# Grouped 1x1 convolution on one core: VectorE block transposes and an in-place ring in place of TensorE transposes and two rings

## The chip, the cores and the metric

The kernel runs on one core of one Trainium2 chip. The metric is the device time of one execution in microseconds (us). Executions of one kernel mostly agree closely: the four of the kernel before took 491.78 to 493.43 us. So differences of 1% are visible when several rounds are run. A run more than 1.5% above the fastest of the same kernel counts as slow. Only fast runs are compared.

The engines are PE (TensorE; PEld is its weight load), DVE (VectorE), ACT (ScalarE), POOL (GpSimd) and SP (the queue that issues loads). A trailing q, as in ACTq, is an engine's sequencer.

## The reference

Every pixel has 192 channels in 4 groups of 48. Each group is multiplied by its own 48x48 matrix. With k = 1 there is no padding and no sum over neighbours:

```python
H = W = 512; G = 4; Cg = 48; C = 192; k = 1
x: (1, 512, 512, 192) bfloat16      w: (1, 1, 4, 48, 48) bfloat16
out = einsum('bhwgc,gcd->bhwgd', x.reshape(1, 512, 512, 4, 48), w[0, 0])
```

The input is 100.66 MB and the output as much. A "column" below is 128 pixels, one per partition: 49,152 bytes in and as many out; there are 2048 columns.

## The kernel before

Pixels lie on partitions. The kernel contracts over partitions, so it first brings the channels there. TensorE does it, by multiplying with an identity; DVE copies the result from PSUM to SBUF; a second set of matmuls multiplies by the weights; ACT (and DVE for one eviction in eight) brings the output to SBUF. Work goes in groups of 4 columns. Loads and stores go in pieces of 64 columns, smaller ones at head and tail. Input and output each have a ring of 256 columns.

```python
BIG = 64; RCOLS = 256
HEAD = (4, 4, 8, 16, 32); TAIL = (32, 16, 8, 4, 4)
...
x_sb = sbuf_tensor([128, RCOLS * C]); o_sb = sbuf_tensor([128, RCOLS * C])
...
for p in loads:                                  # SP
    wq.wait(t_done, p.g1 - body)                 # the slot's old input is transposed
    sp.dma_start(ring_view(x_sb, p), rows_view(xf, p))
...
pe.transpose(xT_ps[:, g % NXP, j * 128:(j + 1) * 128], x_sb[:, col:col + 128], ident[:])   # 6 a group
dve.tensor_copy(xT_sb[g % NXP][:], xT_ps[:, g % NXP, 0:2 * UC])
pe.matmul(o_ps[:, v % NOB, c0_:c1_], lhsT=xs[:, j * 128:(j + 1) * 128], rhs=wt[...])       # 6 a group
...
wait_out_free(wq, g)                             # the slot's old output is stored
act.copy(dst, o_ps[:, v % NOB:v % NOB + 2, 0:UC])
```

## Time and profile before

| | before |
|---|---|
| time, median | 492.5 us |
| span of the profiled run | 489.8 us |
| bytes moved | 201.63 MB |
| GB/s from 100 to 400 us | 431 |
| PE / DVE / ACT busy | 86 / 69 / 73% |

These lines are from the page of the kernel before: busy us of each engine, GB/s in 40 equal slices of the span, the DMA total, and the costliest groups of instructions. A group's line gives the source line, engine and operation, what was written from what, the count, then busy us and mean ns of one, then the engine's idle time just before them and what ended it.

```profile
PE 423.4 (86%) x6154; PEld 407.9 (83%) x6154; DVE 336.1 (69%) x640; ACT 357.2 (73%) x513; POOL 1.3 (0%) x8
...
GB/s 297 430 425 423 428 430 433 427 435 425 436 425 432 433 431 433 429 432 431 425 433 430 429 435 429 434 429 433 429 429 426 438 421 434 421 424 351 238 385 149
DMA packets 11750, 201.63 MB, mean 412 GB/s; under 512 B 1488, under 2 KB 2512, under 8 KB 3536
...
L277 ACT CAST o_sb<-o_ps 128x768 bf16<-128x768 f32 x385 | 301.7, 799 | 116.8 <-PE o_ps L215 68.4
L249 DVE COPY xT_sb<-xT_ps 128x768 bf16<-128x768 bf16 x512 | 284.0, 555 | 111.4 <-PE xT_ps L192 104.4
L215 PE MATMUL o_ps<-wt,xT_sb 128*128 128x144 bf16 (+1 forms) x3072 | 308.2, 238 | 47.9 <-ACT o_sb L277 44.8
L192 PE MATMUL xT_ps<-ident,x_sb 128*128 128x128 bf16 x3072 | 265.7, 225 | 7.8 <-DMA x_sb<-in_x_dram 7.3
...
L255 DVE CAST o_sb<-o_ps 128x384 bf16<-128x384 f32 x127 | 69.8, 550 | 28.0 <-DMA out_dram<-o_sb 26.7
```

After its first slice the GB/s row is flat at about 430 until its last four slices: this kernel is bound by DMA nearly all the way. The chain of waits says the same; this is its summary by line:

```profile
by line: DMA out_dram<-o_sb 73.5%; PE o_ps L215 10.3%; PE xT_ps L192 7.7%; DMA x_sb<-in_x_dram 3.7%; ACT o_sb L277 1.1%; another core or an unknown queue 0.8%; issue 0.6%; SPq L164 0.4%; ACTq L264 0.1%; SPq L161 0.1%; ACTq L46 0.0%
```

The next lines are stretches of the trace before. The columns are the stretch, then for each engine busy us and number of instructions, then the granted TensorE clock, the DMA engines' mean busy share, and GB/s.

```profile
core 0: us, PE busy (x) PEld busy (x) DVE busy (x) ACT busy (x) POOL busy (x), PEclk, DMA share, GB/s
0.00:20.00 20.00, 14.93 (x176) 13.79 (x177) 10.34 (x19) 8.77 (x12) 1.31 (x8) 1.00 0.90 348
100.00:400.00 300.00, 259.70 (x3767) 251.51 (x3765) 206.01 (x393) 217.73 (x315) 0.00 (x0) 0.95 1.00 431
400.00:440.00 40.00, 36.26 (x535) 35.14 (x533) 29.09 (x57) 30.54 (x45) 0.00 (x0) 0.96 1.00 426
440.00:450.00 10.00, 10.00 (x158) 9.76 (x156) 8.36 (x17) 9.00 (x14) 0.00 (x0) 1.00 0.96 399
450.00:460.00 10.00, 9.27 (x143) 8.85 (x141) 8.23 (x16) 8.70 (x13) 0.00 (x0) 1.00 0.80 335
460.00:470.00 10.00, 9.65 (x149) 9.40 (x149) 7.46 (x15) 8.15 (x12) 0.00 (x0) 1.00 0.43 180
470.00:480.00 10.00, 5.88 (x71) 5.26 (x69) 3.53 (x7) 4.61 (x7) 0.00 (x0) 0.85 0.77 323
```

201.63 MB at 431 GB/s take 468 us. The rest of the span is lost in the first 20 us and after 440 us. In that tail PE is nearly always busy until 473 us. Two lines of the same kernel's timeline of PE (start us, duration us, instruction, and in brackets the idle time before it) show: PE stood still for 3.94 us at the very end, for a load.

```profile
472.74 0.58 PE L215 MATMUL o_ps<-wt,xT_sb 128*128 128x144 bf16 x6
477.25 0.82 PE L192 MATMUL xT_ps<-ident,x_sb 128*128 128x128 bf16 x6 [3.94 <-DMA x_sb<-in_x_dram]
```

### The profile page before, as it was taken

The page shows a single profiled execution, that of the slowest core. Times are in us where ns is not written, and L with a number is a line of the kernel's source. Part 1 is how long each engine was busy: PE and PEld are TensorE (multiplying, and loading weights), DVE is VectorE, ACT ScalarE, POOL GpSimd, SP SyncE. Part 2 cuts the span into 40 slices and gives each one's busy share as a digit, 9 for nine tenths or more (in the row PEclk, how much of TensorE's full clock was granted, in tenths as well). Part 3 has the DMA queues.
Part 4 walks back from the last instruction along what each step waited for, and adds up shares of the span by engine and source line. Part 5 has one row for each costly group of instructions (what it writes and reads, how often), then busy time and mean ns, then how long its engine had stood idle before and what let it go on. Part 6 is the DMA issues. An engine that isn't in the chain of part 4 may idle for free.

```text
span 489.8 us, 14171 instructions
## 1 busy us (share of the span) xinstructions
PE 423.4 (86%) x6154; PEld 407.9 (83%) x6154; DVE 336.1 (69%) x640; ACT 357.2 (73%) x513; POOL 1.3 (0%) x8
## 2 busy tenths in 40 slices
PE   5999989977997979979798979899798979799962
PEld 5899989977987879878788878898787978799862
DVE  3688878867675767757676757767577757588750
ACT  2788878866785767767677757678586868688862
POOL 1000000000000000000000000000000000000000
PEclk9999999999898998989998989989899989899996
DMA  8999999999999999999999999999999999998593
GB/s 297 430 425 423 428 430 433 427 435 425 436 425 432 433 431 433 429 432 431 425 433 430 429 435 429 434 429 433 429 429 426 438 421 434 421 424 351 238 385 149
DMA packets 11750, 201.63 MB, mean 412 GB/s; under 512 B 1488, under 2 KB 2512, under 8 KB 3536
## 3 DMA queue, kind: packets, MB, share of 16 engines
q1 hardware_dynamic: 5968, 100.68, 48.3%
q10 hardware_dynamic: 5760, 100.67, 48.2%
q8 instruction: 12, 0.20, 0.1%
q14 instruction: 10, 0.08, 0.0%
HBM read 100.68 MB, written 100.66 MB: 411 GB/s over the span
## 4 chain that ended last, share of the span: by engine, by line
DMA 77%; PE 18%; ACT 1%; another core or an unknown queue 1%; issue 1%; SPq 1%; ACTq 0%
DMA out_dram<-o_sb 73%; PE o_ps L215 10%; PE xT_ps L192 8%; DMA x_sb<-in_x_dram 4%; ACT o_sb L277 1%; SPq L164 0%; ACTq L264 0%; SPq L161 0%; ACTq L46 0%
## 5 line engine op out<-in xcount | busy, mean ns | idle before, releaser
L277 ACT CAST o_sb<-o_ps 128x768 bf16<-128x768 f32 x385 | 301.7, 799 | 116.8 <-PE o_ps L215 68.4
L249 DVE COPY xT_sb<-xT_ps 128x768 bf16<-128x768 bf16 x512 | 284.0, 555 | 111.4 <-PE xT_ps L192 104.4
L215 PE MATMUL o_ps<-wt,xT_sb 128*128 128x144 bf16 (+1 forms) x3072 | 308.2, 238 | 47.9 <-ACT o_sb L277 44.8
L192 PE MATMUL xT_ps<-ident,x_sb 128*128 128x128 bf16 x3072 | 265.7, 225 | 7.8 <-DMA x_sb<-in_x_dram 7.3
L215 PEld LDWEIGHTS o_ps<-wt,xT_sb 128*128 128x128 bf16 x3072 | 217.8, 100 | 61.4 <-issue 52.5
L192 PEld LDWEIGHTS xT_ps<-ident,x_sb 128*128 128x128 bf16 x3072 | 205.6, 101 | 9.5 <-DMA x_sb<-in_x_dram 7.6
L255 DVE CAST o_sb<-o_ps 128x384 bf16<-128x384 f32 x127 | 69.8, 550 | 28.0 <-DMA out_dram<-o_sb 26.7
L274 ACT CAST o_sb<-o_ps 128x384 bf16<-128x384 f32 x127 | 61.0, 480 | 8.0 <-PE o_ps L215 5.1
L245 DVE CAST wt<-o_ps 128x480 bf16<-128x480 f32 x1 | 0.7, 658 | 3.2 <-PE o_ps L176 3.2
L176 PE MATMUL o_ps<-w_sb,esel 48*128 48x48 bf16 x10 | 0.6, 210 | 2.6 <-DMA w_sb<-in_w_dram 2.6
L176 PEld LDWEIGHTS o_ps<-w_sb,esel 48*128 48x128 bf16 x10 | 0.5, 112 | 2.5 <-POOL esel L150 2.5
L277 ACT ACT_TABLE_LOAD x1 | 1.3, 1283 | 0.8 <-PEq L300 0.8
L150 POOL TENSOR_SCALAR_AFFINE_SELECT esel<-esel 48x272 bf16<-48x272 bf16 x1 | 0.4, 406 | 0.0
L147 POOL MEMSET esel<- 48x272 bf16 x1 | 0.3, 318 | 0.3 <-POOLq L300 0.3
L154 POOL TENSOR_SCALAR_AFFINE_SELECT ident<-ident 128x128 bf16<-128x128 bf16 x1 | 0.3, 285 | 0.0
L148 POOL MEMSET ident<- 128x128 bf16 x1 | 0.2, 198 | 0.0
L300 POOL MEMSET const-bfloat16-1.0<- 128x1 bf16 x1 | 0.1, 102 | 0.0
L300 POOL MEMSET const-uint8-127<- 128x1 uint8 x1 | 0.1, 102 | 0.0
L300 POOL MEMSET const-float32-0.0<- 128x1 f32 x1 | 0.1, 98 | 0.3 <-issue 0.3
L300 POOL MEMSET const-float32-1.0<- 128x1 f32 x1 | 0.1, 98 | 0.0
## 6 DMA issues: line engine op xcount, KB each, us to landing
x_sb<-in_x_dram SPq DMA_DIRECT2D x30, 3072.0 KB, 25.7
out_dram<-o_sb ACTq DMA_DIRECT2D x30, 3072.0 KB, 45.4
x_sb<-in_x_dram SPq DMA_DIRECT2D x2, 1536.0 KB, 19.7
out_dram<-o_sb ACTq DMA_DIRECT2D x2, 1536.0 KB, 24.9
x_sb<-in_x_dram SPq DMA_DIRECT2D x2, 768.0 KB, 21.5
out_dram<-o_sb ACTq DMA_DIRECT2D x2, 768.0 KB, 20.0
x_sb<-in_x_dram SPq DMA_DIRECT2D x4, 192.0 KB, 27.2
x_sb<-in_x_dram SPq DMA_DIRECT2D x2, 384.0 KB, 24.4
```

The costliest lines, as they stand in the source:

```text
L147: gp.memset(esel[:], 1.0).then_inc(p0_sem, 1)
L150: gp.affine_select(out=esel[:], in_=esel[:], pattern=[[-1, ECOLS]], compare_op=AluOpType.is_equal, fill=0.0, base=ESHIFT, channel_multipli ...
L154: gp.affine_select(out=ident[:], in_=ident[:], pattern=[[-1, 128]], compare_op=AluOpType.is_equal, fill=0.0, base=0, channel_multiplier=1) ...
L176: last = pe.matmul(o_ps[:, NOB - 1, col:col + CG], lhsT=esel[:, s0:s0 + 128], rhs=w_sb[:, g, :], start=True, stop=True, skip_group_check=True)
L192: ins.append(pe.transpose(xT_ps[:, g % NXP, j * 128:(j + 1) * 128], x_sb[:, col:col + 128], ident[:]))
L215: ins.append(pe.matmul(o_ps[:, v % NOB, c0_:c1_], lhsT=xs[:, j * 128:(j + 1) * 128], rhs=wt[:, WOFF[tc]:WOFF[tc] + (c1_ - c0_)], start=(tc ...
L245: dve.tensor_copy(wt[:], o_ps[:, NOB - 1, 0:WCOLS]).then_inc(wc_sem, 1)
L249: dve.tensor_copy(xT_sb[g % NXP][:], xT_ps[:, g % NXP, 0:2 * UC]).then_inc(e1_sem[g % RING], 1)
L255: dve.tensor_copy(o_sb[:, u * UC:(u + 1) * UC], o_ps[:, v % NOB, 0:UC]).then_inc(d2_sem[g // 4 % 2], 1)
L274: ins = act.copy(o_sb[:, u * UC:(u + 1) * UC], o_ps[:, v % NOB, 0:UC])
L277: ins = act.copy(dst, o_ps[:, v % NOB:v % NOB + 2, 0:UC])
L300: nc = _bacc.Bacc("TRN2", target_bir_lowering=False, num_devices=1)
```

## The change

The intent was to take the transposes off TensorE and their PSUM evictions off DVE. DVE transposes 32x32 blocks from SBUF to SBUF. The kernel is laid out for blocks that stay within 32 partitions, so that each quarter of the partitions keeps its own pixels. The weights therefore become block-diagonal, one copy per quarter, and the 128 PSUM partitions come to mean "pixel run i*4+u". For a store to see those partitions in address order, the transposed columns must be ordered (i, u): the transpose writes its 32 outputs of a block four elements, 8 bytes, apart. Outputs overwrite their inputs in one ring of 512 columns, and a load waits for the store 512 columns earlier.

```diff
-BIG = 64
-RCOLS = 256
-HEAD = (4, 4, 8, 16, 32)
-TAIL = (32, 16, 8, 4, 4)
+STEP = 8
+BIG = 128
+RCOLS = 512
+HEAD = (8, 8, 16, 32, 64)
+TAIL = (64, 32, 16, 8, 8)
 ...
+            for p in pieces:                                    # SP
+                for q in pieces:
+                    if q.col < p.col + p.size - RCOLS and q.col + q.size > p.col - RCOLS:
+                        wq.wait(st_sem[q.i], 16)
+                sp.dma_start(region(p), pixels(xf, p).rearrange("(p i) c -> p (i c)", p=128))
 ...
-                        ins.append(pe.transpose(xT_ps[...], x_sb[:, col:col + 128], ident[:]))
-                    dve.tensor_copy(xT_sb[g % NXP][:], xT_ps[:, g % NXP, 0:2 * UC])
+                src = columns(s).rearrange("p u g (b j) -> p u (g b) j", j=Q)           # Q = 32
+                dst = xT[s % NXT][:].rearrange("p (b i u) -> p u b i", u=NQ, i=Q)       # NQ = 4
+                dve.transpose(dst, src).then_inc(t_done, 1)
 ...
+                for gh in range(4):                             # PE: 12 matmuls a step
+                    for b, o, r in ((1, ...), (0, ...), (2, ...)):
+                        pe.matmul(o, lhsT=xs[:, at:at + 128], rhs=r, start=(b == 1), stop=(b == 2))
 ...
+                dst = pixels(of, p).rearrange("(a q g) c -> q a (g c)", a=NQ, q=128)    # store: 4 runs
+                src = region(p).rearrange("p (a n) -> p a n", a=NQ)                     # a partition
+                act.dma_start(dst, src).then_inc(st_sem[p.i], 16)
+                act.copy(columns(s)..., o_ps[...])              # output over its input
```

## The prediction

> What bounds it now. DMA, then a compute tail. The stretches of the trace show 431 GB/s from 100 to 400 us, DMA share 1.00, and the chain of waits is 73% out_dram<-o_sb. The page counts 201.63 MB; at 431 GB/s that is 468 us of the 489.8 us span. The other 22 us: about 4 us in the first 20 us (348 GB/s) and about 17 us after 440 us (399, 335, 180, 323, 170 GB/s in 10 us stretches). In that tail the loads are over and the chain is PE alone, 6 transposes (0.33 us) and 6 matmuls (0.41 to 0.47 us) per group of 4 columns, 0.78 us a group until 473 us. The backlog exists because compute had been held back by the full output ring (ACT waited 46.9 us and DVE 26.7 us for stores), so about 40 loaded groups were left uncomputed when loads ended.
>
> What the change does, per step of 8 columns (1024 pixels; 256 steps). DMA needs 0.786 MB / 431 GB/s = 1.83 us.
> - Removed: 12 TensorE transposes and two PSUM-to-SBUF copies on DVE (555 ns each), shared evictions (550 ns).
> - DVE: one transpose of 128x1536 bf16. No such instruction is in the trace. [...] 256 x 1.78 = 456 us: DVE goes from 69% to about 95% busy and nearly ties with DMA.
> - PE: 12 matmuls, 3072 columns; the trace's pace (960 columns in 0.41 us) gives 1.32 us, 338 us in all.
> - ACT: one eviction of 128x1536. From 480 ns for 384 and 799 for 768, 1.44 us, 368 us in all. Two PSUM halves: (1.32+1.44)/2 is far under 1.83, so no PSUM stall.
> - In-place ring: the output overwrites the input, so compute never waits for a store; only loads do (store of the piece 512 columns earlier). Bytes unchanged.
>
> On the critical path. The middle stays DMA-bound (no gain). The gain is the tail: compute follows the loads closely, some 280 columns wait in the store queue when loads end, and they drain at DMA rate while the last 100 to 250 columns are computed. I expect the tail's loss to fall from 17 us to about 5, while the head costs 1 to 4 us more (first piece twice as large, weights built by four small DMAs and four ACT copies before the first matmul). Span: 468 + 4 + 5 = 477 us, plus 2 to 3 us between span and time: 480 us, ratio 0.974.
>
> Chances: faster 0.60, same 0.24, slower 0.16; 80% range 474 to 500.
>
> What would show it. DVE transposes of about 1.78 us, DVE over 90% busy; ACT mean 1.44 us; PE under 75%; no ACT or DVE wait for out_dram; 425 to 433 GB/s in the middle, and over 350 GB/s in all but the last 10 us. If DVE is the limit instead, GB/s falls evenly below 425 in the middle, and the chain is DVE transposes.
>
> What would make it wrong. A transpose over 1.85 us (its output is scattered with an 8-byte step[...], this trace shows nothing of it): each 0.1 us is 26 us. A lower DMA rate from 12 KB store runs and 48 KB row pitch. Piece-wise starvation of a DVE with only about 3% slack. Late weights holding DVE after its four buffers.

In the line on DVE the sum came to 1.78 us for one transpose, 1.7 to 1.85 us from start to start. The 1.78 us, and with it the 456 us, the 95% and the 3% of slack, stand as the author's estimate, with no measurement behind it. The sum of the span, 468 + 4 + 5 = 477 us, assumes that DVE keeps up with DMA, but has no term for it.

## The result, and the profile after

| | before | after |
|---|---|---|
| time, median | 492.5 us | 896.8 us |
| span of the profiled run | 489.8 us | 895.0 us |
| ratio of the fast runs | 1 | 1.821 (1.818 to 1.824) |
| DVE busy | 69% | 98% |
| PE busy | 86% | 50% |

A ratio is the mean time of one kernel's fast runs over the mean of the other's in the same rounds, so it is not quite the ratio of the medians. The change is much slower, not 2.6% faster. These lines of the page after answer to those of before:

```profile
PE 445.0 (50%) x3072; PEld 290.0 (32%) x3072; DVE 874.9 (98%) x256; ACT 371.2 (41%) x261; POOL 1.9 (0%) x6
...
GB/s 385 427 413 252 211 71 388 106 282 282 141 385 38 351 212 192 362 10 389 174 236 327 53 396 114 282 282 97 396 70 299 264 149 133 1 281 1 192 186 185
...
L138 DVE STREAM_TRANSPOSE xT<-ring 128x1536 bf16<-128x1536 bf16 x256 | 874.9, 3635 | 14.0 <-PE o_ps L160 10.2
L160 PE MATMUL o_ps<-wt,xT 128*128 128x192 bf16 (+1 forms) x3072 | 445.0, 303 | 445.4 <-DVE xT L138 412.2
L190 ACT CAST ring<-o_ps 128x1536 bf16<-128x1536 f32 x256 | 367.9, 1438 | 510.7 <-PE o_ps L160 488.7
```

The mean of one transpose is 3635 ns, and 874.9 us busy for 256 of them is 3.42 us from one start to the next. (Where DVE never idles, busy time over count is the time from start to start; adjacent instructions overlap a little, so it is below the mean.) The author's estimate was 1.78 us. The chain of waits by line and the longest waits tell one story, that everything waits for DVE; a wait's columns are total us, number of times, longest us:

```profile
by line: DVE xT L138 91.8%; issue 3.1%; ACTq L184 2.5%; PE o_ps L160 0.8%; DVEq L90 0.6%; ACT ring L190 0.5%; DMA ring<-in_x_dram 0.3%
```

```profile
ACT ring L190 <- PE o_ps L160: 488.7, 250, 3.2
...
PE o_ps L160 <- DVE xT L138: 412.2, 246, 1.9
...
DVE xT L138 <- PE o_ps L160: 10.2, 1, 10.2
```

256 x 3.42 us are 875 us. The rest of the 895 us span is 3.7 us before the first transpose, 10.2 us in which DVE waited for PE, and the last step's matmuls, eviction and store. DMA falls to 211 GB/s in the middle, because it has nothing more to do:

```profile
0.00:60.00 60.00, 22.99 (x132) 14.95 (x132) 51.34 (x15) 16.07 (x14) 1.93 (x6) 0.76 0.98 413
60.00:100.00 40.00, 25.61 (x157) 16.60 (x158) 34.68 (x11) 20.93 (x15) 0.00 (x0) 0.76 0.79 320
100.00:400.00 300.00, 182.81 (x1056) 114.53 (x1054) 300.00 (x88) 127.10 (x89) 0.00 (x0) 0.76 0.51 211
```

The 10.2 us have a cause of their own. These are lines of ACT's timeline after: one store's issue took 23.44 us where others took 0.38 us. ACT stood still for 22.05 us with it; PE waited up to 19.4 us for ACT to evict its PSUM, and DVE 10.2 us for PE to free a buffer.

```profile
22.98 0.38 ACTq L184 DMA_DIRECT2D out_dram<-ring  x1
...
37.50 23.44 ACTq L184 DMA_DIRECT2D out_dram<-ring  x1
60.98 2.78 ACT L190 CAST ring<-o_ps 128x1536 bf16<-128x1536 f32 x2 [22.05 <-issue]
```

In the first 60 us the two queues (q1 loads, q10 stores) moved this (packets, MB, share):

```profile
q1 hardware_dynamic: 1122, 24.48, 96.5%
q10 hardware_dynamic: 614, 0.29, 1.7%
```

Load packets are some 22 KB each here (24.48 MB over 1122), store packets about 0.5 KB (0.29 MB over 614; the weights' packets are among them).

### The profile page after: what moved, and what is told of

Same layout as the page of the kernel before. It is cut to its first block, busy times and chain, and to the rows that moved or that the text cites. A ratio compares the mean times of both kernels' runs of the same rounds, so it can differ in the third digit from the quotient of the medians.

```text
span 895.0 us, 7034 instructions
## 1 busy us (share of the span) xinstructions
PE 445.0 (50%) x3072; PEld 290.0 (32%) x3072; DVE 874.9 (98%) x256; ACT 371.2 (41%) x261; POOL 1.9 (0%) x6
## 4 chain that ended last, share of the span: by engine, by line
DVE 92%; issue 3%; ACTq 2%; PE 1%; DVEq 1%; ACT 0%; DMA 0%
DVE xT L138 92%; ACTq L184 2%; PE o_ps L160 1%; DVEq L90 1%; ACT ring L190 0%; DMA ring<-in_x_dram 0%
## 5 line engine op out<-in xcount | busy, mean ns | idle before, releaser
L138 DVE STREAM_TRANSPOSE xT<-ring 128x1536 bf16<-128x1536 bf16 x256 | 874.9, 3635 | 14.0 <-PE o_ps L160 10.2
L160 PE MATMUL o_ps<-wt,xT 128*128 128x192 bf16 (+1 forms) x3072 | 445.0, 303 | 445.4 <-DVE xT L138 412.2
L190 ACT CAST ring<-o_ps 128x1536 bf16<-128x1536 f32 x256 | 367.9, 1438 | 510.7 <-PE o_ps L160 488.7
L160 PEld LDWEIGHTS o_ps<-wt,xT 128*128 128x128 bf16 x3072 | 290.0, 107 | 600.2 <-DVE xT L138 474.8
L176 ACT COPY wt<-w_sb 32x384 bf16<-32x384 bf16 x4 | 2.0, 510 | 0.1
```

Source lines behind the costliest of these rows:

```text
L138: dve.transpose(dst, src).then_inc(t_done, 1)
L160: ins = pe.matmul(o, lhsT=xs[:, at:at + 128], rhs=r, start=(b == 1), stop=(b == 2), skip_group_check=True)
L176: act.copy(dst, w_sb[:]).then_inc(wc_sem, 1)
L190: act.copy(dst, src).then_inc(o_done, 1)
```

## The experiments

Two questions were open. Why does a transpose cost 3.42 us? And would the rest of the prediction have held, had it cost what was expected? The first seven experiments, all on the transpose, and the one on the head after them give a wrong result, since moving columns about spoils the matmul's order; the bytes moved and the work of the other engines are those of a real run. The diffs below show only the lines that matter.

### The transpose: step, operation, size

**Unit step.** The only edit is the order of the output columns:

```diff
-dst = xT[s % NXT][:].rearrange("p (b i u) -> p u b i", u=NQ, i=Q)
+dst = xT[s % NXT][:].rearrange("p (u b i) -> p u b i", u=NQ, i=Q)
```

> Edit: the transpose writes its output in one contiguous run (order u, b, i) instead of with an 8-byte step; the result is wrong on purpose. Theory S[...]: the transpose falls from 3.4 us start to start to about 1.8 us and the time to about 480 to 500 us. Theory T[...]: stays within 3% of 3.4 us, time about 895 us.

Theory S lays the 3.4 us on the step of the output; theory T lays it on the 32x32 transpose of 2-byte elements, whatever its patterns.

Time 497.9 us (one run). The group of DVE in this run:

```profile
L138 DVE STREAM_TRANSPOSE xT<-ring 128x1536 bf16<-128x1536 bf16 x256 | 425.8, 1736 | 42.9 <-PE o_ps L160 36.0 <-DMA ring<-in_x_dram 6.9
```

425.8 us over 256 is 1.66 us, 1.08 ns per element, where the change took 3.42 us, 2.22 ns. Theory T, that a transpose takes the longer time whatever its pattern, falls. The output's step is what doubled the cost.

**A plain copy with the change's own patterns.**

```diff
-dve.transpose(dst, src).then_inc(t_done, 1)
+dve.tensor_copy(dst, src).then_inc(t_done, 1)
```

> Edit: a plain DVE copy with the very same source and destination patterns in place of the transpose; wrong result on purpose. Theory S: about 3.4 us each, time about 895 us. Theory T: about 1.6 to 1.8 us each[...], and the time then shows what the rest of the change is worth with a DVE instruction of the predicted size: the prediction's 480 us if its account of the ring and the tail is right, more if they cost something.

Time 500.2 us (one run).

```profile
L138 DVE COPY xT<-ring 128x1536 bf16<-128x1536 bf16 x256 | 442.0, 2044 | 39.4 <-PE o_ps L160 34.1 <-DMA ring<-in_x_dram 5.2
```

1.73 us each, 1.12 ns per element. So the plain form of theory S falls as well: a copy that writes 8 bytes apart takes about as long as the transpose with a unit step. It takes the step and the transpose together.

**Half of the blocks**, with the same 8-byte step:

```diff
-src = columns(s).rearrange("p u g (b j) -> p u (g b) j", j=Q)
-dst = xT[s % NXT][:].rearrange("p (b i u) -> p u b i", u=NQ, i=Q)
+src = columns(s)[:, :, 0, :].rearrange("p u (b j) -> p u b j", j=Q)
+dst = xT[s % NXT][:, 0:XT // 2].rearrange("p (b i u) -> p u b i", u=NQ, i=Q)
```

> Edit: each step transposes only the first of its two pixel groups, 24 of 48 blocks, 768 elements per partition, with the same 8-byte step; wrong result on purpose. [...] If half of the 3.4 us were a fixed cost of one instruction, about 2.6 us. With DVE at about 1.8 us, the time tests the rest of the prediction: 480 us if it is right.

The forecast, for a cost that goes by elements, was about 1.8 us start to start.

Time 501.1 us (one run).

```profile
L141 DVE STREAM_TRANSPOSE xT<-ring 128x768 bf16<-128x768 bf16 x256 | 440.4, 1915 | 40.2 <-PE o_ps L164 34.4 <-DMA ring<-in_x_dram 5.8
```

1.72 us for 768 elements against 3.42 us for 1536: 1.70 us for 768 more, 2.21 ns per element, which leaves 0.02 us fixed. (This run also zeroes the unused half of each buffer once, at the start.)

**The same bytes as 4-byte elements:**

```diff
-src = columns(s).rearrange("p u g (b j) -> p u (g b) j", j=Q)
-dst = xT[s % NXT][:].rearrange("p (b i u) -> p u b i", u=NQ, i=Q)
+src = region(piece_of[s]).bitcast(F32)...rearrange("p u g (b j) -> p u (g b) j", j=Q)
+dst = xT[s % NXT][:].bitcast(F32).rearrange("p (b i u) -> p u b i", u=NQ, i=Q)
```

> Edit: the same bytes transposed as 768 4-byte elements (pairs of channels stay together; wrong result on purpose, as the matmuls are not adapted). [...]: about 1.8 us. If the cost goes by bytes: about 3.4 us. [...]: about 1.0 us. The output's step grows from 8 to 16 bytes[...].

Two forecasts are for an element that costs as much at 4 bytes as at 2 (1.8 us), and for one that costs half as much (1.0 us); theory S expected no less than the first.

Time 497.9 us (one run).

```profile
L140 DVE STREAM_TRANSPOSE xT<-ring 128x768 f32<-128x768 f32 x256 | 376.1, 1556 | 87.8 <-PE o_ps L162 39.4 <-DMA ring<-in_x_dram 37.8
```

Here DVE waits for others, so busy over count, 1.47 us, is an upper bound. Ten in a row span 13.99 us in the trace; less the last one's own 1.56 us (the mean), that is 1.38 us from start to start, some 1.80 ns for each of 768 elements. The step is 16 bytes here, and a 4-byte element costs less than a 2-byte one at 8 bytes (2.22 ns). None of the three expectations fits exactly, and the distance in bytes alone does not explain the cost.

**A step of 2 elements**, 4 bytes (u split into v and w, output ordered b, v, i, w):

```diff
+src = columns(s).rearrange("p (v w) g (b j) -> p v w (g b) j", v=2, j=Q)
+dst = xT[s % NXT][:].rearrange("p (b v i w) -> p v w b i", w=2, v=2, i=Q)
```

> Edit: the transpose writes its output with a step of 2 elements (4 bytes) in place of 4 (8 bytes); wrong result on purpose. Found so far: 1.66 us start to start with step 1, 3.42 us with step 4, a plain copy with step 4 1.72 us. Theory U[...]: 3.4 us, time about 895 us. Theory L (the cost follows how far apart consecutive writes lie[...]): clearly less than 3.4 us, between 1.7 and 2.6 us, time 500 to 700 us.

Theory U is that only a unit step is fast, and any other costs as much as the step of 4.

Time 502.3 us (one run); 446.7 us over 256 is 1.74 us, 1.14 ns per element. A unit step is not needed; theory U falls.

```profile
L138 DVE STREAM_TRANSPOSE xT<-ring 128x1536 bf16<-128x1536 bf16 x256 | 446.7, 1918 | 39.7 <-PE o_ps L160 34.5 <-DMA ring<-in_x_dram 5.0
```

**A step of 8 elements**, 16 bytes, for the transpose and for the plain copy:

```diff
+src = columns(s)...rearrange("p u (c e) j -> p u c e j", e=2)
+dst = xT[s % NXT][:].rearrange("p (c i e u) -> p u c e i", e=2, u=NQ, i=Q)
```

> Edit: the transpose writes with a step of 8 elements (16 bytes), in the patterns of the change otherwise; wrong result on purpose. Known: step 1 1.66 us start to start, step 2 1.74 us, step 4 3.42 us. If the cost doubles[...]: near 6.5 us, time near 1700 us. [...]: 3.4 us, time about 895 us.

> Edit: a plain copy with the step of 8 elements (16 bytes) in place of the transpose; wrong result on purpose. The copy took 1.72 us at a step of 4 elements. If a step of more than 4 elements slows every DVE write, and the transpose only has half the tolerance: about 3.4 us, time about 895 us. If the step matters to the transpose alone: 1.7 us, time about 500 us.

The forecast for the transpose, 3.4 us, is for one that loses no more beyond a step of 8 bytes.

The transpose ran in 1756.0 us, the copy in 896.7 us (one run each).

```profile
L138 DVE STREAM_TRANSPOSE xT<-ring 128x1536 bf16<-128x1536 bf16 x256 | 1743.1, 7181 | 3.8 <-DMA ring<-in_x_dram 3.8
```

```profile
L138 DVE COPY xT<-ring 128x1536 bf16<-128x1536 bf16 x256 | 874.8, 3848 | 13.9 <-PE o_ps L160 10.4 <-DMA ring<-in_x_dram 3.6
```

The runs on 2-byte elements give one table, start to start for 1536 elements per partition:

| output step | transpose | plain copy |
|---|---|---|
| 1 (2 bytes) | 1.66 us | not run |
| 2 (4 bytes) | 1.74 us | not run |
| 4 (8 bytes) | 3.42 us | 1.73 us |
| 8 (16 bytes) | 6.81 us | 3.42 us |

The transpose's cost doubles from a step of 2 to 4 and again to 8; the copy's doubles only from 4 to 8. Of the steps that were run, the change's is the first at which the transpose lost. What in the hardware makes it so was not tested.

### The head: what separates 498 from 480 us

With a fast transpose the kernel still took 498 us. All five runs with a transpose or copy of at most 1.74 us and the fine head took 498 to 502 us, and in each of their traces one store issue of 31 to 34 us stands in the first 65 us. The theory was the blocked issue of a store: the head's small pieces make small store packets, which wait among large load packets. The edit keeps the unit step and makes the head coarser:

```diff
-HEAD = (8, 8, 16, 32, 64)
+HEAD = (64, 64)
```

> Edit: contiguous transpose output (as in the first experiment, wrong result on purpose) and the head pieces 8, 8, 16, 32, 64 columns replaced by two of 64. There the fourth small store's issue held ACT for 32 us, DVE then waited 36 us, and the time was 498 us. Theory H (many small store descriptors behind large load packets block the issue of the next store; that is what separates 498 from the predicted 480): no ACT issue over 5 us, DVE idle under 15 us in all, time 478 to 486 us. Rival R (the in-place ring of 512 columns loses the time anyway, because loads fill it and then wait for the starved stores): time stays at 494 to 500 us.

482.9 us, median of 4 runs, ratio to before 0.982 (0.981 to 0.984). With the fine head, one line of ACT's timeline and DVE's wait for PE:

```profile
28.67 32.37 ACTq L184 DMA_DIRECT2D out_dram<-ring  x1
```

```profile
DVE xT L138 <- PE o_ps L160: 36.0, 3, 30.8
```

With the coarse head no store issue of the first 150 us took over 0.41 us, and the same wait is

```profile
DVE xT L138 <- PE o_ps L160: 9.4, 2, 8.6
```

The stretches of the run with the fine head, and then with the coarse one, show where the time went; the last number is GB/s:

```profile
60.00:100.00 40.00, 35.85 (x274) 24.79 (x275) 33.73 (x21) 34.10 (x24) 0.00 (x0) 0.90 0.81 328
100.00:200.00 100.00, 89.97 (x730) 60.69 (x729) 100.00 (x61) 87.41 (x62) 0.00 (x0) 1.00 0.95 390
...
400.00:470.00 70.00, 60.67 (x493) 40.99 (x492) 66.68 (x41) 58.95 (x41) 0.00 (x0) 1.00 1.00 423
```

```profile
60.00:100.00 40.00, 36.22 (x298) 24.77 (x297) 40.00 (x25) 35.56 (x25) 0.00 (x0) 1.00 0.95 383
100.00:200.00 100.00, 89.29 (x723) 59.99 (x721) 100.00 (x62) 86.54 (x62) 0.00 (x0) 1.00 1.00 428
...
400.00:450.00 50.00, 43.00 (x348) 28.99 (x348) 49.76 (x30) 41.08 (x29) 0.00 (x0) 1.00 1.01 428
450.00:470.00 20.00, 4.49 (x37) 3.00 (x36) 3.47 (x3) 5.76 (x4) 0.00 (x0) 0.72 1.00 424
```

With the fine head, compute stood still for 31 us, and DMA ran below its rate until 200 us. Theory H's forecast of the time holds, and rival R falls: the 512-column ring does not cost those 15 us. Two of H's side forecasts missed: DVE still idled 28 us in all, of which 11.0 us went to the larger first load, and a store's issue once more held ACT, for 7.9 us, in the tail, once DVE had finished, while the stores ran on at 424 GB/s. The run changes the size and the number of the head's pieces at once, so it does not tell which of the two matters. The run also shows the tail that the prediction counted on: after DVE has finished, stores run on at 424 GB/s, and only the last 11 us are below. How the DMA engines share their time between queues was not measured; in the first 60 us of the change, the queue with packets of some 0.5 KB moved 0.29 MB beside the 24.48 MB of the one with packets of some 22 KB. That the blocked issue comes from a full store queue is an inference; it was not measured by itself.

### The other half of the change alone

The in-place ring can be had with TensorE transposes:

```diff
-RCOLS = 256
+RCOLS = 512
-o_sb = sbuf_tensor("o_sb", ...)
+o_sb = x_sb
-wq.wait(t_done, p.g1 - body)
+for q in stores: (wait for those that overlap p.col - RCOLS)
```

> Edit: the kernel before, with its TensorE transposes, but with the other half of the change: one in-place ring of 512 columns in place of two rings of 256; loads wait for the store 512 columns earlier, compute never waits for a store. Theory (the prediction's account of the tail): the tail after the last load stays at over 400 GB/s until the last 10 us, time 474 to 484 us, 2 to 4% faster than before, correct. Rival (loads flood the queue first and the starved stores cost at the head what the tail gives): 488 to 495 us, with a GB/s dip between 40 and 100 us.

Correct, 492.2 us, ratio 0.9997 (0.9975 to 1.0018): no gain. Compute no longer waits for stores, but PE stood still for the last small loads, as its timeline shows:

```profile
464.10 0.82 PE L192 MATMUL xT_ps<-ident,x_sb 128*128 128x128 bf16 x6 [5.23 <-DMA x_sb<-in_x_dram]
...
472.02 0.82 PE L192 MATMUL xT_ps<-ident,x_sb 128*128 128x128 bf16 x6 [4.86 <-DMA x_sb<-in_x_dram]
...
479.84 0.82 PE L192 MATMUL xT_ps<-ident,x_sb 128*128 128x128 bf16 x6 [6.20 <-DMA x_sb<-in_x_dram]
```

From 440 us on, only 0.89 MB of loads were left, in 438 packets (about 2 KB each), while 14.45 MB of stores went out in 1245 packets (about 12 KB each). So the next two runs replaced the loads' small tail by whole pieces, with the in-place ring and without it:

```diff
-loads = plan_pieces(cols, HEAD, TAIL)
+loads = plan_pieces(cols, HEAD, ())
```

> Edit: the in-place ring with TensorE transposes as before, and the loads' tail of 32, 16, 8, 4, 4 columns replaced by whole 64-column pieces (stores keep their tail). In the in-place run with the small tail loads, these landed only at 464, 472 and 480 us behind large store packets, and PE waited for each. Theory M (small load packets starve behind large store packets at the end, as small stores do behind large loads at the head): time 475 to 483 us, about 3% faster than before, with DMA over 400 GB/s until about 470 us. Rival (the in-place ring has no tail to give): 488 to 494 us.

> Edit: the kernel before, two rings of 256 columns, with only the loads' tail replaced by whole 64-column pieces. Tells whether the gain of the run above comes from the in-place ring or from the tail pieces alone. If the compute backlog behind the full output ring makes the tail (the prediction's account): 488 to 494 us, no gain. If the small tail loads made it: 475 to 484 us.

Both results are wrong in the tail (relative error 0.25): a piece's size decides which pixel lies on which partition, and the tail's loads and stores no longer agreed. The bytes and the work are the same, so the times still count: 490.6 us, ratio 0.996 (0.993 to 0.999), and 492.2 us, ratio 0.9996. Theory M as a forecast of time missed: with the in-place ring the loads did land earlier (446.7 us) and PE was done by 464 us, but the span was still 488.6 us. With two rings they landed at 447.5 us, yet PE had work without a wait for a load until 478 us. That fits the backlog behind the output ring that the prediction described; but doing without that ring gained no more than 0.4%.

The trace's records of semaphore updates show one more reason. There are 16 for one DMA, as many as the page counts DMA engines; each is read here as the landing of one engine's share. These are the updates of one DMA each, in us:

```
before, last load:              441.2 441.4 441.4 441.7 442.6 442.8 442.8 442.9 443.0 443.0 443.1 451.8 452.4 453.0 453.2 477.2
in place, whole loads, last store: 470.2 470.2 470.5 470.9 471.1 472.4 475.4 478.4 479.0 479.2 480.0 480.0 480.3 480.4 481.3 488.1
unit step, coarse head, last store: 476.1 476.7 476.7 476.8 477.2 477.4 477.5 478.0 478.5 478.7 479.1 479.2 479.5 479.8 479.9 480.8
```

In the kernel before, one share of the last load came 24 us after the others. In these two kernels with TensorE transposes one share lags; in the third all come within 5 us. It is not a matter of TensorE transposes, though: in the two-queue version below, which has none, the shares of the last load came from 446.6 to 481.3 us. So the tail of before is not only the compute backlog that the prediction read. Why one share lags was not settled.

### Can a correct version have the fast transpose?

A build with the order restored at the matmul's stationary operand was refused ("exactly one free dimension"). So in the versions here the order of the transposed columns is the order of the PSUM partitions; their results are correct. With a unit step that order is (u, i), and a piece is stored here by four DMAs of 32 partitions each:

```diff
+dst = xT[s % NXT][:].rearrange("p (b u i) -> p u b i", u=NQ, i=Q)
+HEAD = (64, 64)
+dst = pixels(of, p).rearrange("(a i u g) c -> u i a (g c)", a=NQ, i=Q, u=NQ)
+for u in range(NQ):
+    act.dma_start(dst[u], src[u * Q:(u + 1) * Q]).then_inc(st_sem[p.i], 16)
```

> Edit: a correct version with unit-step output: within each 32-channel block the transposed columns are ordered (u, i), so a PSUM partition holds pixel run u*32+i, and each piece is stored by four DMAs, one per u, of 32 partitions each; two head pieces of 64 columns. If only the output's step made the change slow: correct result, transposes 1.65 to 1.75 us start to start, time within 2% of the run with the coarse head alone (480 to 492 us), against 895. Rival: stores of 32 partitions each run slower than 128-partition ones, and the DMA rate falls below 415 GB/s in the middle, time over 500 us.

Correct, but 619 and 627 us in its two fast runs, ratio 1.267; two more runs were slow. In the profiled run, a slow one, the middle ran at 332 GB/s, and the four store issues of a piece together held ACT for up to 17.6 us. With a step of two elements, two DMAs of 64 partitions are enough, once each load brings two runs per partition in place of one:

```diff
+dst = pixels(of, p).rearrange("(v a q g) c -> v q a (g c)", v=2, a=NQ, q=64)
+eng.dma_start(dst[v], src[v * 64:(v + 1) * 64])        # ACT issues both
```

> Edit: a correct version with an output step of 2 elements (1.74 us a transpose): PSUM partition = v*64 + i*2 + w, u = (v, w); each piece loaded as two runs per partition and stored by two DMAs of 64 partitions each, both from ACT's queue; head pieces 64, 64. Theory P (a store that covers only some of the partitions at a time has less than full rate): better than the 335 GB/s of four 32-partition stores or the same, but below 400 GB/s in the middle; time 520 to 630 us. Rival (it was the number of DMAs and their descriptors that made those slow): two DMAs bring 480 to 492 us.

Correct, 557.9 us in its one run that counts as fast (three slow ones to 587 us). The same, with the second half issued by GpSimd so that both are under way:

```diff
+@block.gpsimd:  for p in pieces: wait o_done; half_store(gp, p, 1)
```

> Edit: as e15, but the second store of each piece (partitions 64 to 127) is issued from GpSimd's queue, so both halves are under way at once. Theory P: all partitions are covered again, 425 GB/s in the middle, correct, time 482 to 492 us. Rival: as e15, or slower if GpSimd's queue itself is slow.

Correct, 492.6 us, ratio 0.998 (0.994 to 1.002). The stretch from 100 to 400 us in the three runs, in that order; the last number is GB/s:

```profile
100.00:400.00 300.00, 216.38 (x1619) 151.73 (x1617) 224.62 (x135) 190.02 (x135) 0.00 (x0) 0.86 0.99 332
```

```profile
100.00:400.00 300.00, 215.68 (x1716) 151.19 (x1714) 248.45 (x143) 202.41 (x144) 0.00 (x0) 0.92 1.00 369
```

```profile
100.00:400.00 300.00, 252.13 (x2007) 170.96 (x2006) 291.36 (x168) 240.07 (x168) 7.01 (x11) 0.98 1.01 424
```

Theory P's forecast holds: with both halves under way the rate is back at 424. In the two others the DMA engines were occupied just as fully (share 0.99 and 1.00) and moved less. Stores of 64 and of 32 partitions at a time went with 369 and 332 GB/s, all 128 under way with 424. These rates contain the loads too, and the two lower ones are from traces of slow runs, so they do not measure what a store of some of the partitions costs; why it moves less was not shown. A rival stays open: the last version has a second store queue as well as all partitions under way, and two queues that share the same partitions were not tried.

Three more runs, all correct, went after its head and tail: weights loaded behind the first piece with a head of 32, 32, 64 columns; then tails of 64, 64 and of 64, 32, 32.

```diff
-HEAD = (64, 64)                 +HEAD = (32, 32, 64)     # and weights on SP's queue
-TAIL = (64, 32, 16, 8, 8)       +TAIL = (64, 64)         # then (64, 32, 32)
```

> Edit: as e13, and the four weight loads go out on the loads' queue right behind the first piece, with head pieces 32, 32, 64. In the run with the coarse head, weights landed at 20 us and the first matmul was at 23.5 us. Expected: first matmul before 13 us, and if e13 reaches DMA rate, 3 to 8 us less than e13, 476 to 486 us; if e13 is bound by slow stores, no difference over 2%.

> Edit: the correct version with early weights, tail pieces 64, 32, 16, 8, 8 replaced by 64, 64. Theory M (small load packets starve behind large store packets): the last load lands before 458 us in place of 482, DVE is done by about 470 us, time 480 to 486 us. Rival: the tail's length is set by the DMA engines' own imbalance, and nothing changes (490 to 496 us).

> Edit: the same with tail pieces 64, 32, 32: smaller last store, but smaller load packets. Theory M: last load between the two others, 458 to 470 us; time 482 to 490 us. Rival: 490 to 496 us.

They took 494.5, 497.4 (one of its six runs slow) and 491.0 us; the ratios are 1.004, 1.010 and 0.996 (0.993 to 0.999). All three missed the gain that was hoped for. The first matmul came at 11.4 us instead of 16.9 us, and the last load was in at 458 us (coarse tail) and 461 us (middle tail) instead of 482 us. As a cause theory M held, as a gain it did not: DVE then ran without a gap until 472 us and 477 us, and at 1.74 us a step, beside the 1.83 us that DMA needs, it had hardly any slack to catch up. No correct version beat the kernel before by 2%; the best, by 0.4%, is not worth its complexity.

One way was left untested: 4-byte elements. That transpose took at most 1.47 us and keeps the order that lets one DMA store all 128 partitions; only the matmuls were not adapted. An estimate from the counts speaks against it: a block of 32 channel pairs always touches two groups of 48 channels, so a step would have 12 matmuls of 384 columns, 4608 in place of 3072, and at the coarse-head run's 1.49 us for 3072 (381.6 us of PE over 256 steps) PE would need some 2.2 us a step, more than DMA's 1.83.

## Why the prediction was wrong

- **The step that failed, the cost of one transpose:** "DVE: one transpose of 128x1536 bf16. No such instruction is in the trace." The author's estimate was 1.78 us. It measured 3.42 us. The estimate is near what an output step of 1 or 2 elements takes (1.66 and 1.74 us), but the change's step of 4 takes about twice that. 256 x (3.42 - 1.78) us are 420 us, more than the whole difference of 404 us between 896.8 and 492.5 us.
- **The risk was named and then discounted.** The prediction said that the output is scattered with an 8-byte step, and discounted it. A plain copy does keep 1.12 ns per element at 8 bytes (1.73 us); a transpose takes 2.22 ns (3.42 us), and from 8 to 16 bytes both lose a factor of two (to 3.42 and 6.81 us).
- **The head was mis-sized.** "The head costs 1 to 4 us more" left out that the head's stores had become runs of 768 to 6144 bytes, four to a partition. In the run with the unit step, the fine head cost 15 us more than a coarse one (497.9 against 482.9 us). The sum 468 + 4 + 5 carried only the 4 us that the kernel before lost in its first 20 us, and not the 1 to 4 us more.
- **The rest held as a sum.** With a unit step and a coarse head, neither of which the prediction had, and at a wrong result, the kernel took 482.9 us, where 480 us had been predicted. ACT's eviction was 1438 ns (predicted 1.44 us), compute never waited for a store, and the tail lost about 4 us (some 11 us at 285 instead of 431 GB/s; predicted 5). PE was priced too low: 1.49 us a step against 1.32, 79% busy where under 75% had been said. That this did no harm was luck: DVE and DMA needed longer still.
- **Its reading of the tail before was only part of the truth.** "In that tail the loads are over" was wrong: the last load's last share landed at 477.2 us. Taking the output ring's back-pressure away and keeping the TensorE transposes gained nothing (ratio 0.9997), and with whole loads only 0.4%.
- **The order of the PSUM partitions was the hidden price.** The 8-byte step was there to let one DMA store all 128 partitions. The versions that gave it up paid in stores: with 1.74 us transposes the best was 491.0 us, and only with two store queues.

## What to carry to other kernels

Before pricing a VectorE transpose, look at the step of its output: here 1536 2-byte elements per partition took 1.66 and 1.74 us at steps of 1 and 2 elements and 3.42 us at 4, where a plain copy still took 1.73 us; measure it in a run of its own. Where loads and stores share the DMA engines, look at the head for a queue of small packets that hardly moves (here 0.29 MB beside 24.48 MB in 60 us) and for an issue that holds up its engine (23.44 us here, 32.37 us in the run with the unit step): coarser head pieces were worth 15 us here, coarser tail pieces at most 0.4%. When one layout choice serves two masters, here the transpose's output and the store, price both sides of it.
